# Outer products of one chunk moved behind the first products, two loads swapped, and last groups issued in two rounds

## The chip, the cores and the metric

The kernel runs on one core of a Trainium2 chip. The metric is the device time of one execution in microseconds (us). The engines of the core are TensorE (PE, matrix products and weight loads), VectorE (DVE), ScalarE (ACT), GpSimd (POOL) and SyncE (SP, which here only issues DMA transfers). Each takes its own instructions strictly in the order of the program and waits on semaphores of the others. Products are summed in PSUM, which is divided into eight banks.

## The reference

A linear attention with decay (a retention recurrence), followed by a two-layer network with the Mish function between the layers:

```python
# q, k, v: (4 batches, 8 heads, 768 steps, 64)
for t in range(S):
    state = gamma[None, :, None, None] * state + np.einsum('bhd,bhe->bhde', k[:, :, t], v[:, :, t])
    y[:, :, t] = scale * np.einsum('bhd,bhde->bhe', q[:, :, t], state)
# x: (3072 tokens, 512); w_in: (512, 2048); w_out: (2048, 512)
h = x @ w_in
sp = np.where(h > 20.0, h, np.log1p(np.exp(np.minimum(h, 20.0))))
g = h * np.tanh(sp)
return (g @ w_out).astype(np.float32)
```

Inputs and output are float32; the kernel works on float16 copies and sums in float32.

## The kernel before, in words

**Chunks and blocks.** The recurrence is computed in 24 chunks of 128 steps (six per batch). Within a chunk the scores of k and q are formed, masked on DVE to the causal half and multiplied by v ("present", L303 and L469); what came before enters through a state, the decayed sum of the outer products of k and v, multiplied by q ("past", L314 and L452). The chunks are grouped in blocks: the first block has four chunks (512 tokens), each further one two (256 tokens). A block's attention output is copied by ACT into a tile `xt`, and then goes through both layers: first products with `w_in` into `h_ps`, Mish on ACT, second products with `w_out` into `o_ps`. From the second block on both layers use seven products for eight, with sums formed on DVE (`x_sums`, `sums_a`, `hsum`, `gsum`, `tmat`).

**The first block** (`first_block`) works on pairs of chunks with two interleaved tokens in each partition, so that one chunk's tokens lie in 64 of the 128 partitions: chunk 0 (or 2) in the lower half, chunk 1 (or 3) in the upper. `outer_first(s)` forms the outer products of both chunks of pair s with 16 products of 64 rows, the two chunks by turns (L291), into one PSUM tile `u_ps` for each chunk. `state_first(g)` adds the previous state with a product by the identity (L299) and lets DVE multiply by the decay (L301), which gives the state of chunk g. `first_g1(h_ps, u, s)` computes half (256 tokens) of the first product u, four products of 128x256 each (L810). Products 0 to 3 take the first slice of `w_in` and are done by halves, so that the first halves can start once the first two chunks' `xt` is there; products 4 to 15 are whole (`g1`, L527).

**Weights.** Each of `w_in` and `w_out` comes in four slices of 1 MB in float32 (`load_w`), in staging tiles of which there are few; a staging tile is loaded anew when its casts are done. `cast_win` (L174) and `cast_wout` (L182 on DVE, L184 on ACT) make the float16 copies. The casts of `w_in` slices 1 to 3 stand on DVE behind the state of chunk 3. The last slice of `w_out` comes in two halves (`load_last_wout`, L168), behind the q and v of chunks 4 and 5 in the order in which SP issues. The staging tiles' release makes SP wait: the second slice of `w_out` needs the tile of `w_in` slice 1.

**Order.** The order of each engine's instructions is the order in which the code issues them (a manual schedule). PSUM tiles with the tag "mm" share four banks; a new tile takes a bank that an earlier one has given up, and its first product waits for that tile's last reader. Tiles with the tag "at" share the other two slots of two banks each.

**The end of the first block** (`first_g2`) forms four output groups, one per chunk, in four PSUM tiles (`t0[0]`, `t1[0]`, `t0[1]`, `t1[1]`). `end(p, i, half)` adds to a group the products of half of the last slice of `w_out` (L1009, two products of 128x512), and `ended(p, i)` adds on DVE (L1015, L1017) and copies on ACT (L1018) what goes to the output. `y_two(1, False)` forms the attention output of the second block, whose `xt` ACT copies at L512, and `outer_two(1)` the outer products that the next blocks need. What follows is the first layer of the second block (`g1_seven`, L642 and L666), for which four sums `x_sums` (L615 to L618) are made on DVE.

Of the kernel before, what the change touches and what calls it, by code (L numbers as in the profile page):

```python
# [10 lines left out]
FP32 = mybir.dt.float32  # L11
# [5 lines left out]
def kernel(  # L17
# [9 lines left out]
    nc = tc.nc  # L27
    B, H, S, D = q.shape
    d_model, d_ff = moe_w_in.shape
    P = 128  # L30
# [3 lines left out]
    HP = H // 2  # L34
    TB = 512
    CPB = TB // C
# [7 lines left out]
    FPS = NFB // NSL  # L44
# [24 lines left out]
    mmps = ctx.enter_context(  # L69
        tc.tile_pool(name="rn_mmps", bufs=4, space=bass.MemoryType.PSUM))  # L70
# [46 lines left out]
    raw, k16s, v16s, t16s, kts, amf = {}, {}, {}, {}, {}, {}  # L117
# [18 lines left out]
    def load_one(g, n, queue):  # L136
        b, c = divmod(g, NCH)
        queue.dma_start(
            loaded[g][n], (q, k, v)[n][b, :, c * C:(c + 1) * C].rearrange("h p d -> p h d"))
# [26 lines left out]
    def load_last_wout(half):  # L166
        f = slice(half * (FPS // 2), (half + 1) * (FPS // 2))
        nc.sync.dma_start(  # L168
            wtmps["out", NSL - 1][:, f], wout_ap[:, NFB - FPS + f.start:NFB - FPS + f.stop])
# [91 lines left out]
    def toks(c):  # L261
        return slice(c * HB, (c + 1) * HB)
# [19 lines left out]
            tri_first.rearrange("p r t -> p (r t)").unsqueeze(1).broadcast_to(  # L282
                (P, HP, R * C)), op=ALU.mult)

    def outer_first(s):
        us[s] = [mmps.tile([P, HP, P], FP32, name="u_ps", tag="mm") for _ in range(2)]
        for i in range(HP):
            half, j = divmod(i, HP // 2)
            for r in range(R):
                for c in range(2):  # L290
                    nc.tensor.matmul(  # L291
                        us[s][c][:, i], k16s[s][toks(c), half, r, 2 * j:2 * j + 2],
                        v16s[s, half][toks(c), r, 2 * j:2 * j + 2],
                        start=i == 0 and r == 0, stop=r == R - 1, skip_group_check=True)

    def state_first(g):
        u = us[g // 2][g % 2]
        if g > 0:
            nc.tensor.matmul(u, ident, states[g - 1], start=False, stop=True, skip_group_check=True)  # L299
        states[g] = stp.tile([P, HP, P], FP16, name="st")  # L300
        nc.vector.tensor_tensor(states[g], u, gcm, op=ALU.mult)  # L301
# [192 lines left out]
    def outer_two(blk):  # L494
        gs = handed_on(blk)
        if gs:
            u_ps = u_tile()
        for j, g in enumerate(gs):
            outer(g, u_ps[:, j, :, :D])
# [35 lines left out]
    def mish(blk, u, h_ps):  # L535
        nt = BLOCKS[blk] * C
        per = TB // nt
        room = NFB * TB // (2 * nt)
        at0, lies = divmod(u * per, room)
        if lies == 0:  # L540
            gtiles[blk, at0] = gp.tile([P, room, nt], FP16, name="g", tag="g0" if blk == 0 else "g")
        gt = gtiles[blk, at0][:, lies:lies + per]
        nc.scalar.activation(gt, h_ps, AF.Mish, scale=inv_boost3)
        for j in range(per):
            gts[blk, u * per + j] = gt[:, j]
# [244 lines left out]
    def load_weights():  # L790
        for s in range(NSL):
            load_w("in", s)
        for s in range(NSL):
            load_w("out", s)
        room(CPB)
        room(CPB + 1)
        for g in (CPB, CPB + 1):
            load_one(g, 0, nc.sync)
            load_one(g, 2, nc.sync)

    def load_more():
        load_last_wout(0)
        load_last_wout(1)
        nload[0] += 2
        load_to(CPB + 4)

    def first_g1(h_ps, u, s):
        t = slice(s * TB // 2, (s + 1) * TB // 2)
        for bp in range(NBP):
            nc.tensor.matmul(  # L810
                h_ps[:, 0, t], win(0, u, bp), xts[0][:, 2 * s:2 * s + 2, bp],
                start=bp == 0, stop=bp == NBP - 1, skip_group_check=True)

    def first_block():
        qf = load_first_q()
        for s in range(2):
            for nm in "kv":
                for half in range(2):
                    load_two(nm, s, half)
        nload[0] = CPB  # L820
        load_weights()
        xts[0] = xtp.tile([P, CPB, HP, C], FP16, name="xt")

        at = at_tile()
        spin_wide(at, HP)
        spin_wide(at, HP)
        spin(at, 8)
        tq = turn_first_q(qf, 0)
        spin_wide(at, 3)
        first_q_out(0, tq, nc.scalar)  # L830
        tq = [tq, turn_first_q(qf, 1)]
        cast_two("k", 0, 0)
        turn_two(0, 0)
        first_q_out(1, tq[1], nc.vector)
        turned_two(0, 0)
        cast_two("k", 0, 1)
        spin_wide(at, 3)
        scores_half(0, 0, at)
        mask_half(0, 0, at)
        turn_two(0, 1)  # L840
        turned_two(0, 1)
        for half in range(2):
            cast_two("v", 0, half)
        at = at_tile()
        spin_wide(at, 3)
        scores_half(0, 1, at)
        mask_half(0, 1, at)
        cast_two("k", 1, 0)
        turn_two(1, 0)
        turned_two(1, 0)  # L850
        cast_two("k", 1, 1)
        outer_first(0)
        state_first(0)
        at = at_tile()
        scores_half(1, 0, at)
        mask_half(1, 0, at)
        y = atps.tile([P, 2, HP, C], FP32, name="y_ps", tag="at")
        present_first(0, y, range(HP))
        turn_two(1, 1)
        turned_two(1, 1)  # L860
        state_first(1)
        past_first(1, y)
        xt_out(0, y)
        for half in range(2):
            cast_two("v", 1, half)
        cast_win(0, 0, nc.gpsimd)
        at = at_tile()
        scores_half(1, 1, at)
        mask_half(1, 1, at)
        y = atps.tile([P, 2, HP, C], FP32, name="y_ps", tag="at")  # L870
        outer_first(1)
        state_first(2)
        h_ps = [mmps.tile([P, 1, TB], FP32, name="h_ps", tag="mm") for _ in range(2)]
        present_first(1, y, range(HP))
        first_g1(h_ps[0], 0, 0)
        past_first(2, y)
        past_first(3, y)
        xt_out(2, y)
        first_g1(h_ps[1], 1, 0)
        cast_win(0, 1, nc.vector)  # L880
        state_first(3)
        for u in range(2, FPS):
            h_ps.append(mmps.tile([P, 1, TB], FP32, name="h_ps", tag="mm"))
            first_g1(h_ps[u], u, 0)
        for u in range(FPS):
            first_g1(h_ps[u], u, 1)
            mish(0, u, h_ps[u])
        for s in range(1, NSL):
            for half in range(2):
                cast_win(s, half, nc.vector)  # L890
            if s == 2:
                late.extend(win_sums())
            if s >= 2:
                some_late(4)
        room_for_sums()
        late.extend(weight_sums(0) + weight_sums(1))
        plan = {9: [(cast_wout, 0), (room_for_more,), (bring_first,)],
                10: [(some_late, 1)],
                12: [(g_sum, 1), (g_sum, 2), (cast_wout, 1), (room_for_more,), (g_sum, 3)],
                16: [(load_more,)]}  # L900
        for u in range(FPS, NFB):
            g1(0, u)
            for fn, *args in plan.get(u + 1, ()):
                fn(*args)
        first_g2()
        hsnaps.append(gp.tile([P, 4, TB], FP32, name="hsnap", tag="g0"))

# [20 lines left out]
    def first_g2():  # L928
        hf = d_model // 2
        pairs = range(CPB // 2)  # L930
# [76 lines left out]
        def end(p, i, half):  # L1007
            for f in range(2 * half, 2 * half + 2):
                nc.tensor.matmul(  # L1009
                    (t0, t1)[i][p], a(p, i, 3)(f), wouts[3][:, f], start=False,  # L1010
                    stop=f == FPS - 1, skip_group_check=True)

        def ended(p, i):
            if i == 0:
                nc.vector.tensor_tensor(osb[p][0], t0[p], osb[p][0], op=ALU.add)  # L1015
            else:
                nc.vector.tensor_tensor(osb[p][1][:, 1], pz[p], osb[p][1][:, 1], op=ALU.add)  # L1017
                nc.scalar.copy(osb[p][1][:, 0], px[p])  # L1018
            row0 = (2 * p + i) * P
            stores.append((1, out[row0:row0 + P], osb[p][i].rearrange("p j c -> p (j c)")))  # L1020

        end(0, 0, 0)
        end(0, 1, 0)
        end(0, 0, 1)
        ended(0, 0)
        end(0, 1, 1)
        ended(0, 1)
        y_two(1, False)
        for half in range(2):
            end(1, 0, half)  # L1030
        ended(1, 0)
        outer_two(1)
        for half in range(2):
            end(1, 1, half)
        ended(1, 1)

    def turn_and_load(g):
        if g < NCK:
# [95 lines left out]
```

## Time and profile before

| | |
|---|---|
| median of 3 runs | 200.24 us (200.23 to 200.88) |
| the profiled execution's own time | 199.78 us |
| its span, first to last instruction | 197.8 us |
| granted TensorE clock | 1.00 |
| PE busy | 189.3 us (96%) |
| DVE / ACT / POOL busy | 143.2 / 105.5 / 91.7 us |
| mean DMA rate | 182 GB/s; about 385 GB/s from 18 to 30 us |

All times in the text are counted from the first instruction of the span. The last chain of work, followed back from the end, lies on PE for 86% of the span. A product's row in the timeline has a modelled end, so the spacing of products is read from their starts. The issue of a DMA and its landing are two things: a landing is the last update of the transfer's semaphore.

### The profile page before, as it was taken

Reading aid. Unit: us, or ns where it says so; the run is one execution under the profiler, and the core shown is the slowest. Engines: PE = TensorE matmul, PEld = TensorE weight load, DVE = VectorE, ACT = ScalarE, POOL = GpSimd, SP = SyncE. Lnnn points to the kernel's source line nnn. Section 1 sums busy time; section 2 is a strip of 40 time slices with the busy share of each in tenths; the row PEclk is TensorE's granted clock in tenths of the full one; section 3 lists DMA queues with packets and bytes.
Section 4 is the critical chain, followed back from the end, with each engine's and each line's share of the span. In section 5 each row is a group of like instructions: output and inputs, shape, how many; then the busy total and the mean of one; then the engine's idle time right before and its main releaser. Section 6 shows DMA issues by size and latency. Waiting matters only on the chain.

```text
span 197.8 us, 5839 instructions
## 1 busy us (share of the span) xinstructions
PE 189.3 (96%) x2431; PEld 157.2 (79%) x2431; DVE 143.2 (72%) x293; ACT 105.5 (53%) x191; POOL 91.7 (46%) x125
## 2 busy tenths in 40 slices
PE   6797999999999999999999999999999999999992
PEld 2355645885988988988988988988988988988982
DVE  3786699778897697597498597597498596596362
ACT  3464577444663663663663753753753753753840
POOL 4072006597663929719707809808716814110000
PEclk9999999999999999999999999999999999999999
DMA  5999999999999999999999995996997974101102
GB/s 170 303 311 376 383 388 302 191 300 165 157 195 204 260 220 210 156 153 214 195 174 111 200 174 128 167 174 149 182 182 123 166 125 97 68 2 56 53 30 80
DMA packets 95658, 36.06 MB, mean 182 GB/s; under 512 B 82576, under 2 KB 89232, under 8 KB 95632
## 3 DMA queue, kind: packets, MB, share of 16 engines
q1 hardware_dynamic: 74400, 33.04, 74.8%
q0 software_dynamic: 21088, 2.62, 21.6%
q8 instruction: 19, 0.31, 0.6%
q14 instruction: 7, 0.06, 0.1%
q10 hardware_dynamic: 144, 0.03, 0.1%
HBM read 27.30 MB, written 6.29 MB: 170 GB/s over the span
## 4 chain that ended last, share of the span: by engine, by line
PE 86%; DVE 6%; DMA 2%; ACT 2%; issue 2%; DVEq 0%
PE o_ps L739 29%; PE h_ps L666 17%; PE h_ps L642 15%; PE h_ps L527 5%; PE o_ps L953 5%; PE y_ps L474 3%; PE at L404 3%; DMA qfirst<-in_q_dram 2%; PE o_ps L1009 2%; PE h_ps L810 2%; PE y_ps L465 1%; DVE st L301 1%; PE u_ps L419 1%; DVE am L279 1%; DVE gsum L585 1%
## 5 line engine op out<-in xcount | busy, mean ns | idle before, releaser
L666 PE MATMUL h_ps<-xt,win 128*128 128x256 f16 x320 | 41.6, 273 | 0.0
L659 DVE TENSOR_TENSOR hsum<-h_ps,hsnap 128x512 f32<-128x512 f32 x30 | 19.8, 688 | 20.8 <-PE h_ps L642 16.9
L739 PEld LDWEIGHTS <-gsum 128*128 128x128 f16 x320 | 30.5, 98 | 4.5
L666 PEld LDWEIGHTS <-win 128*128 128x128 f16 x320 | 29.3, 98 | 3.6
L349 POOL DMA_DIRECT2D qk<-in_k_dram x36 | 27.9, 778 | 0.0
L739 PE MATMUL o_ps<-tmat,gsum 128*128 128x256 f16 x240 | 27.9, 273 | 0.0
L739 PEld LDWEIGHTS <-g 128*128 128x128 f16 x240 | 23.4, 98 | 2.8
L653 ACT ACTIVATE g<-hsum 128x512 f16<-128x512 f32 x30 | 18.6, 630 | 11.4 <-DVE hsum L659 11.2
L410 DVE TENSOR_TENSOR am<-at,tri 128x1024 f16<-128x1024 f32 x20 | 24.3, 1216 | 0.0
L673 ACT ACTIVATE g<-h_ps 128x512 f16<-128x512 f32 x40 | 22.8, 599 | 2.4 <-PE h_ps L666 2.4
L354 POOL TENSOR_TENSOR v<-vf,qvs 128x512 f16<-128x512 f32 x20 | 23.5, 1176 | 1.1 <-DMA vf<-in_v_dram 0.7
L745 ACT COPY snap<-o_ps 128x256 f32<-128x256 f32 x30 | 11.2, 373 | 21.7 <-PE o_ps L739 21.6
L649 ACT COPY hsnap<-h_ps 128x512 f32<-128x512 f32 x30 | 16.4, 582 | 11.5 <-PE h_ps L642 11.5
L362 POOL COPY gate<-gsum 128x1 f16<-128x1 f16 x9 | 1.7, 188 | 44.3 <-DVE gsum L713 40.1
L337 POOL TENSOR_TENSOR qk<-qf,qvs 128x512 f16<-128x512 f32 x20 | 21.2, 1062 | 0.7 <-DMA qf<-in_q_dram 0.6
L753 DVE TENSOR_TENSOR osb<-o_ps,snap 128x256 f32<-128x256 f32 x30 | 12.6, 419 | 12.2 <-PE o_ps L739 10.8
L642 PEld LDWEIGHTS <-wsum 128*128 128x128 f16 x320 | 19.5, 98 | 0.5
L739 PE MATMUL o_ps<-wout,g 128*128 128x256 f16 x160 | 19.3, 273 | 0.0
L512 ACT CAST xt<-y_ps 128x1024 f16<-128x1024 f32 x10 | 10.1, 1013 | 14.6 <-PE y_ps L465 14.6
L642 PE MATMUL h_ps<-xsum,wsum 128*128 128x128 f16 x240 | 16.7, 219 | 0.0
L642 PEld LDWEIGHTS <-win 128*128 128x128 f16 x240 | 15.1, 98 | 0.7
L585 DVE TENSOR_TENSOR gsum<-g 128x256 f16<-128x256 f16 (+1 forms) x30 | 10.7, 358 | 3.8 <-ACT g L653 3.6
(120 smaller groups left out, 294.6 us busy)
## 6 DMA issues: line engine op xcount, KB each, us to landing
vf<-in_v_dram SPq DMA_DIRECT2D x24, 256.0 KB, 6.0
out_dram<-osb SPq DMA_DIRECT2D x22, 256.0 KB, 4.6
qf<-in_q_dram SPq DMA_DIRECT2D x20, 256.0 KB, 5.5
wi<-in_moe_w_in_dram SPq DMA_DIRECT2D x3, 1024.0 KB, 11.3
wt<-in_moe_w_out_dram SPq DMA_DIRECT2D x3, 1024.0 KB, 10.9
qk<-in_k_dram POOLq DMA_DIRECT2D x36, 64.0 KB, 4.9
qfirst<-in_q_dram SPq DMA_DIRECT2D x2, 512.0 KB, 5.0
kf<-in_k_dram SPq DMA_DIRECT2D x4, 256.0 KB, 5.8
```

What stands on the lines that cost most here:

```text
L337: nc.gpsimd.tensor_tensor(by_head(g, room16(g)[0]), by_head(0, loaded[g][0]), f.broadcast_to((P, 2, HP, D)), op=ALU.mult)
L349: nc.gpsimd.dma_start(room16(g)[1][:, x::2], src[:, HP * x:HP * x + HP])
L354: nc.gpsimd.tensor_tensor(room16(g)[2], loaded[g][2], vs.unsqueeze(2).broadcast_to((P, H, D)), op=ALU.mult)
L410: nc.vector.tensor_tensor(am, ats.pop(g), tri.unsqueeze(1).unsqueeze(1).broadcast_to((P, 2, HP, C)), op=ALU.mult)
L585: nc.vector.tensor_tensor(s1, a21, a22, op=ALU.add)
L642: nc.tensor.matmul(h_ps[:, f], w(f, d), x(d), start=first and f == 0 and d == 0, stop=d == n - 1, skip_group_check=True)
L649: nc.scalar.copy(x, h_ps)
L653: nc.scalar.activation(gt[:, 2 * i * FPS:(2 * i + 1) * FPS, j * P:(j + 1) * P], h, AF.Mish, scale=inv_boost3)
L659: nc.vector.tensor_tensor(h, h_ps, x, op=ALU.add)
L666: nc.tensor.matmul(h_ps[:, j], win(s, 2 * half + j, bp), xt(blk, bp), start=bp == 0, stop=bp == NBP - 1)
L673: nc.scalar.activation(gt[:, fb:fb + 2], h_ps, AF.Mish, scale=inv_boost3)
L739: nc.tensor.matmul(o_ps, x(f), w(f), start=first and f == 0, stop=f == n - 1, skip_group_check=True)
```

## The change

`outer_first` takes a list of chunks and can form one chunk's outer products alone. For the second pair of the first block, chunk 2's eight products and its state stay where they were; chunk 3's products and state move behind all halves of the first products 0 to 3. Between them the order becomes: present, past of chunks 2 and 3, the copy of `xt`, first halves of products 0 to 3, second halves with their Mish, chunk 3's outer products, its state, and then the casts of the `w_in` slices 1 to 3 as before. Before, the first half of product 0 stood ahead of the past, that of product 1 behind it, then the state of chunk 3, then the halves of products 2 and 3.

Among the loads the first half of the last `w_out` slice changes places with v of chunk 5. At the end of the first block all four groups take the first half of the last slice, then comes `y_two(1, False)`, then all four take the second half and are ended, with `outer_two(1)` between the second and the third.

```diff
-    def outer_first(s):
-        us[s] = [mmps.tile([P, HP, P], FP32, name="u_ps", tag="mm") for _ in range(2)]
+    def outer_first(s, chunks=(0, 1)):
+        u_ps = {c: mmps.tile([P, HP, P], FP32, name="u_ps", tag="mm") for c in chunks}
         for i in range(HP):
             half, j = divmod(i, HP // 2)
             for r in range(R):
-                for c in range(2):
+                for c in chunks:
                     nc.tensor.matmul(
-                        us[s][c][:, i], k16s[s][toks(c), half, r, 2 * j:2 * j + 2],
+                        u_ps[c][:, i], k16s[s][toks(c), half, r, 2 * j:2 * j + 2],
                         v16s[s, half][toks(c), r, 2 * j:2 * j + 2],
                         start=i == 0 and r == 0, stop=r == R - 1, skip_group_check=True)
+        for c in chunks:
+            us[2 * s + c] = u_ps[c]
...
-        for g in (CPB, CPB + 1):
-            load_one(g, 0, nc.sync)
-            load_one(g, 2, nc.sync)
+        load_one(CPB, 0, nc.sync)
+        load_one(CPB, 2, nc.sync)
+        load_one(CPB + 1, 0, nc.sync)
 
     def load_more():
         load_last_wout(0)
+        load_one(CPB + 1, 2, nc.sync)
         load_last_wout(1)
...
-        outer_first(1)
+        outer_first(1, [0])
         state_first(2)
         h_ps = [mmps.tile([P, 1, TB], FP32, name="h_ps", tag="mm") for _ in range(2)]
         present_first(1, y, range(HP))
-        first_g1(h_ps[0], 0, 0)
         past_first(2, y)
         past_first(3, y)
         xt_out(2, y)
-        first_g1(h_ps[1], 1, 0)
         cast_win(0, 1, nc.vector)
-        state_first(3)
-        for u in range(2, FPS):
-            h_ps.append(mmps.tile([P, 1, TB], FP32, name="h_ps", tag="mm"))
+        for u in range(FPS):
+            if u >= 2:
+                h_ps.append(mmps.tile([P, 1, TB], FP32, name="h_ps", tag="mm"))
             first_g1(h_ps[u], u, 0)
         for u in range(FPS):
             first_g1(h_ps[u], u, 1)
             mish(0, u, h_ps[u])
+        outer_first(1, [1])
+        state_first(3)
         for s in range(1, NSL):
             for half in range(2):
                 cast_win(s, half, nc.vector)
...
-        end(0, 0, 0)
-        end(0, 1, 0)
-        end(0, 0, 1)
-        ended(0, 0)
-        end(0, 1, 1)
-        ended(0, 1)
+        ends = [(p, i) for p in pairs for i in range(2)]
+        for p, i in ends:
+            end(p, i, 0)
         y_two(1, False)
-        for half in range(2):
-            end(1, 0, half)
-        ended(1, 0)
-        outer_two(1)
-        for half in range(2):
-            end(1, 1, half)
-        ended(1, 1)
+        for p, i in ends:
+            if (p, i) == (1, 0):
+                outer_two(1)
+            end(p, i, 1)
+            ended(p, i)
```

## The prediction

> **What bounds the kernel now.** I read the page first: the span, the busy shares and the chain that ended last.
>
> ```profile
> span 197.8 us, 5839 instructions
> PE 189.3 (96%) x2431; PEld 157.2 (79%) x2431; DVE 143.2 (72%) x293; ACT 105.5 (53%) x191; POOL 91.7 (46%) x125
> q8 instruction: 19, 0.31, 0.6%
> PE 86%; DVE 6%; DMA 2%; ACT 2%; issue 2%; DVEq 0%
> ```
>
> TensorE (PE) is the bound: whatever makes it wait is paid in full, whatever lies on another engine is paid only if PE waits for it. So I went to the timeline of all engines where the change falls (columns: start, duration, what; in brackets the idle time before it and what ended it).
>
> ```profile
> 15.33 0.62 PE L291 MATMUL u_ps<-v,qk 64*128 64x128 f16 x16
> 16.59 0.68 DVE L301 TENSOR_TENSOR st<-u_ps,gcm 128x512 f16<-128x512 f32 x1
> 17.07 0.61 PE L810 MATMUL h_ps<-xt,win 128*128 128x256 f16 x4
> 17.19 0.68 DVE L174 CAST win<-wi 128x1024 f16<-128x1024 f32 x1
> 17.97 0.27 PE L810 MATMUL h_ps<-xt,win 128*128 128x256 f16 x1
> 19.05 0.49 PE L810 MATMUL h_ps<-xt,win 128*128 128x256 f16 x3 [0.81 <-issue]
> 19.38 0.38 PE L299 MATMUL u_ps<-st,ident 128*128 128x512 f16 x1
> 19.79 0.69 DVE L301 TENSOR_TENSOR st<-u_ps,gcm 128x512 f16<-128x512 f32 x1 [1.92 <-PE u_ps L299]
> 20.54 2.34 PE L810 MATMUL h_ps<-xt,win 128*128 128x256 f16 x20 [0.34 <-DVE st L301]
> 20.74 1.29 DVE L174 CAST win<-wi 128x1024 f16<-128x1024 f32 x2 [0.25 <-DMA wi<-in_moe_w_in_dram]
> 22.72 0.59 PE L527 MATMUL h_ps<-xt,win 128*128 128x512 f16 x2
> ```
>
> Two PE stalls stand here: a start-to-start gap of 1.08 us (17.97 to 19.05, "issue": no semaphore), and one before 20.54, where the fourth product needs the PSUM bank that the state of chunk 3 has just been read from. See also the order on VectorE (DVE): state, then the two casts of weight slice 1, done at 22.03, 0.7 us before L527 needs them at 22.72. From there to 58 us PE has no stall over 0.2 us. Next SyncE's issues, and the stretch at the end of the first block:
>
> ```profile
> 17.95 5.03 SPq L163 DMA_DIRECT2D wt<-in_moe_w_out_dram  x3
> 34.15 0.96 SPq L138 DMA_DIRECT2D vf<-in_v_dram  x1
> 35.16 2.09 SPq L168 DMA_DIRECT2D wt<-in_moe_w_out_dram  x2
> 44.60 1.05 ACT L184 CAST wout<-wt 128x1024 f16<-128x1024 f32 x1 [0.42 <-DMA wt<-in_moe_w_out_dram]
> 44.72 2.00 PE L1009 MATMUL o_ps<-wout,g 128*128 128x512 f16 x8
> ```
>
> The eight products start 0.216 us apart but for the fifth, the first that needs the second half of the last output slice: that half is cast only at 45.65, and the product starts at 45.70 instead of 45.59. This 0.1 us is all that the loading order costs PE.
>
> **What the issue gap is.** PE has 4871 records and queue q8 moved 19 packets, 0.31 MB: 16 KB, so 256 instructions of 64 bytes, each. In the trace the first q8 packet moves at 16.49 to 17.58, when DMA is full (385 GB/s), and the later ones begin where PE's records number about 950, 1250, 1544, 1767: one block of 256 each. The gap falls behind record 448. I read it as a block of instructions landing late, usable at 19.05 whatever is in it. The Trainium skill, "Runtime: NRT & Kernel Launch", Instruction fetch mechanics, says that an engine fetches blocks of 256 instructions by itself and that crossing a block is mostly hidden; the size agrees with the trace, the hiding does not at this place, if my reading holds. By that rule the gap would be something else; that is the first rival.
>
> **The change, part by part.** All from the profiled execution (199.78 us, span 197.8 and 1.98 around it); its time lies 0.46 below the median of 200.24.
>
> *Outer products split.* The 16 products of half rows (64x128) alternate between the two chunks, and start every 28 ns. The eight of chunk 2 alone stay where they were. The trace shows no run of one half alone: low bound 28 ns (0.22 us), high bound 98 ns (a weight load each, 0.78). I take 56 ns, the row of full-height products of the same width (L642, 16 in 0.89): 0.45. For chunk 2 this costs nothing: outer and state product end by 16.1, and present waits for the mask until 16.73 either way. The Trainium skill, "TensorEngine Tiling (Array Packing)", Key Properties, says that different tiles compute in parallel and that each is tied to its partitions; by it one half alone loses the overlap, 0.45 as taken here and not 0.22, and it speaks against this split.
>
> *The new order on PE.* Present ends, next kind starts at 17.07 as before. The past products come at once (8, 0.45: 17.52); xt's second half is copied from about 17.7 to 18.7, before it is needed. Products 0, 1, 2 of first halves: 12 by 0.109, to 18.83. There record 448 is reached again (8 pairs fewer from the outer products, 8 more first halves), and PE waits to 19.05: 0.2 us where 1.08 stood. Product 3 and the second halves: 20 by 0.109, to 21.23. The bank wait of 0.34 is gone. Chunk 3's outer products: a switch of kind (148 ns against 56, so 0.09), 0.45, another 0.09: the state product starts at 21.86. Their bank was one of the four products': product 0's activation ends by 20.8, no wait; if it is product 3's, some 0.6 more (its activation ends at about 22.0). I take the first, free soonest.
>
> *What is late next.* DVE runs in order, and the state of chunk 3 now waits for a product 2.5 us later than before (19.38 to 21.86), with the casts of slice 1 queued behind it. State product to DVE 0.41 (19.38 to 19.79): 22.27. Next DVE instruction 0.60 later (16.59 to 17.19), cast 0.68: 23.55, release 0.05 (20.48 to 20.54): L527 starts at 23.60 instead of 22.72, **+0.88**. With the bounds of the outer products, +0.65 to +1.21.
>
> *Behind the casts.* The casts of slice 2 start 0.6 later; their users on PE come 3.5 us after L527, so hidden; DVE catches up at 34.38 and 36.37, where it idled 0.39 (a DMA) and 1.08 (ScalarE, ACT). SyncE (SP) issues the second output slice only when both casts of slice 1 are done: 22.06 becomes about 24.2. Ahead of it in the queue lie the last input slice (landed 26.1) and the first output slice (28.8), so its landing at 31.55 holds; were that cover gone it would land up to 2.1 later and be cast by 34.9, still ahead of PE's first use of it at 35.7. The q and v loads behind it were held back by a full queue to 34.1 and catch up.
>
> *Loads swapped.* The first half of the last output slice lands about 1.2 us earlier (43.1 to 41.9: v of chunk 5 took 39.34 to 40.50), v of chunk 5 some 2.6 later (40.5 to 43.1). GpSimd (POOL) takes v of chunk 5 at 43.14, now 44.0: hidden by 0.9. The second half lands as before, 44.6.
>
> *Two rounds.* The same products and switches; the second round starts after y_two, 2.9 us later, so the 0.1 wait goes: **-0.10**. The copy of xt leaves from behind the last groups and comes sooner, with nothing waiting for it. On DVE the four sums now follow y_two closely: counted from its end, the fourth starts 2.43 us later instead of 2.27, and xsum 0.16 later. DVE idles 0.24 before 54.01, which hides that. Chunk 3's state is ready 20 us ahead of its next reader (L446, 44.5).
>
> Sum: +0.88 - 0.10 = **+0.78**; nothing behind it gives any back, since PE and the DVE chain of 54 to 62 us both shift. 199.78 becomes 200.56; on the median, 201.0.
>
> **Rivals.**
> 1. *The pause goes with the instructions, not with the clock* (or the block is asked for later): PE stops 1.08 at record 448, so 19.80 instead of 19.05, +0.75 more: 201.8, slower by over 0.5%. Decides once PE resumes after about 19.3. For it: "issue" names no cause. Against: the q8 packets.
> 2. *The casts hold nothing up*: PE goes from the state product (21.86 and 0.22) straight to L527: 22.08, -0.64, with -0.10 and so 199.5, faster. It decides if the casts of slice 1 end before 22.03. For it: the weights landed by 20.7, DVE is idle from 17.9. Against: DVE's rows stand in the order of the code, and there the state stays ahead of the casts.
> 3. *DVE becomes the bound in block 1*: if the third sum waits for ACT's copy (one such wait of 0.5 is listed), xsum is 0.48 late, 0.24 over its cover, and PE, which already waits 0.2 for the mask at 61.95, pays it: 201.3.
>
> **How the numbers follow.** Forecast 0.60, rival 1 0.15, rival 2 0.13, rival 3 0.12. About 0.5% (1.0 us) is what a measurement can tell from no change. The forecast's own range is +0.55 to +1.11: 200.8 to 201.35. The range goes down to 200.1 for the 0.65 by which the three runs differ, and up to 201.9 to take in rivals 1 and 3; it leaves out rival 2 and some ends. Slower by over 0.5% (from 201.24): rival 1, half of rival 3, and 0.10 of the forecast's upper end, 0.31. Faster by over 0.5% (199.24): the lower part of rival 2, 0.05. Within: 0.64.
>
> **What would show it.** L527's first product at 23.6 behind a DVE cast, DVE idle from 17.9 to 22.3, the "issue" gap near 0.2 and ending at 19.05, the bank wait gone; SP's second output slice at 24.2 with its landing unmoved; no gap in L1009; PE's wait at 62 as before. The prediction is wrong if the issue gap is long at another place, if the casts come ahead of the state, or if a wait appears behind 45 us.

## The result and the profile after

The changed kernel takes 201.14 us (median), the kernel before 200.19 us beside it: a ratio of 1.0053 with an interval of [1.0034, 1.0073]. It is slower, by 0.95 us between the medians; 201.0 was predicted. The ratio is of means, without two slow executions of the changed kernel (203.62 and 204.61). The profiled execution of the changed kernel took 200.51 us (span 198.6), the least of its 22; that of the kernel before took 199.78 (span 197.8). That is 0.73 more, where the sum of the prediction was 0.78.

In the new code the lines have moved by two or three: L299 is now L301 (state product), L301 L303 (state on DVE), L527 L529 (whole first products), L642 L644, L666 L668, L739 L741, L810 L813, L1009 L1012, L1017 L1020, L1018 L1021.

The page's first line, and its chain that ended last by engine: the instructions are as many as before, and PE's share of the chain went from 86% to 90%, while "issue" went from 2% to 1%.

```profile
span 198.6 us, 5839 instructions
PE 90%; DVE 3%; DMA 2%; ACT 1%; issue 1%; DVEq 0%
```

The timeline after, PE and DVE, where chunk 3's outer products now stand (start, duration, what, and in brackets the idle time before it and its releaser):

```profile
17.52 3.76 PE L813 MATMUL h_ps<-xt,win 128*128 128x256 f16 x32
21.77 0.39 PE L301 MATMUL u_ps<-st,ident 128*128 128x512 f16 x1
22.19 0.69 DVE L303 TENSOR_TENSOR st<-u_ps,gcm 128x512 f16<-128x512 f32 x1 [4.36 <-PE u_ps L301]
22.80 2.49 DVE L174 CAST win<-wi 128x1024 f16<-128x1024 f32 x4
23.54 0.82 PE L529 MATMUL h_ps<-xt,win 128*128 128x512 f16 x3 [1.39 <-DVE win L174]
```

The 32 half products run as one group from 17.52; the two stalls of before (1.08 at the block of instructions, 0.34 at the bank) have left one start-to-start gap, 18.84 to 19.05, inside that group. But DVE then stands idle for 4.36 us, because the state of chunk 3 is next in its order, and the casts behind it end so late that PE waits 1.39 us in front of L529. PE's two small stalls were traded for one large one.

At the end of the first block the eight products of the first half (L1012) now run from 45.55 without a gap. What follows in the timeline of after (PE, DVE, ACT):

```profile
50.52 1.06 PE L644 MATMUL h_ps<-xt,win 128*128 128x128 f16 x16
50.97 0.41 DVE L1020 TENSOR_TENSOR osb<-o_ps,osb 128x256 f32<-128x256 f32 x1
51.41 0.37 ACT L1021 COPY osb<-o_ps 128x256 f32<-128x256 f32 x1 [0.84 <-DVE osb L1020]
51.68 0.59 ACT L651 COPY hsnap<-h_ps 128x512 f32<-128x512 f32 x1
52.31 0.69 DVE L661 TENSOR_TENSOR hsum<-h_ps,hsnap 128x512 f32<-128x512 f32 x1
57.37 1.04 PE L741 MATMUL o_ps<-wout,g 128*128 128x256 f16 x8
```

The same stretch in the timeline of before, for comparison:

```profile
49.76 1.06 PE L642 MATMUL h_ps<-xt,win 128*128 128x128 f16 x16
49.95 0.42 DVE L1017 TENSOR_TENSOR osb<-o_ps,osb 128x256 f32<-128x256 f32 x1 [0.45 <-PE o_ps L1009]
50.41 0.37 ACT L1018 COPY osb<-o_ps 128x256 f32<-128x256 f32 x1 [0.79 <-DVE osb L1017]
51.31 0.69 DVE L659 TENSOR_TENSOR hsum<-h_ps,hsnap 128x512 f32<-128x512 f32 x1
```

Between the first product of this layer and the first of the next lie 6.62 us before (49.76 to 56.38) and 6.85 after (50.52 to 57.37). Four small gaps make the difference, each before a product whose semaphores wait for DVE or ACT: 0.04 at 52.33, 0.10 at 54.19, 0.04 at 54.68 and 0.055 at 55.17 (of the two groups of eight there, the starts are 0.49 apart where 0.44 stood). `hsum`, the first sum over a finished `h_ps`, starts 1.79 us behind the first L644; before it was 1.55. Both numbers are the start of the last group's sum (0.45 behind the first L644, 0.20 behind the first L642 before) and 1.34 or 1.35 us more. The last sum is late because it follows the third group's sum on DVE without a pause (its row has no idle time), where DVE had idled 0.45 before.

Two ways lead from the last sum to `hsum`, and they are nearly equally long. ACT's copy and then `hsnap` end at 52.28, and `hsum` follows at 52.31. On DVE itself the four x sums stand between; they are spaced about 0.20 us (the last two start at 51.83 and 52.03), so by an estimate DVE alone would have begun `hsum` at 52.23, still 0.16 later against PE than before.

The balance at a product that both share, the fourth group of L741 (62.82 before, 63.69 after): 0.82 at L529, less 0.10 at L1012, plus 0.24 in these gaps, less 0.11 because the wait for the mask at 62 fell from 0.23 to 0.12. That is 0.85 of the 0.87, and the span is 0.8 longer. The next run shows which edit each of these belongs to.

### The profile page after: what moved, and what is told of

Its sections match the earlier page's. It is cut to its first block, busy times and chain, and to the rows that moved or that the text cites. A ratio compares the mean times of both kernels' runs of the same rounds, so it can differ in the third digit from the quotient of the medians.

```text
span 198.6 us, 5839 instructions
## 1 busy us (share of the span) xinstructions
PE 190.6 (96%) x2431; PEld 157.8 (79%) x2431; DVE 143.0 (72%) x293; ACT 105.5 (53%) x191; POOL 91.7 (46%) x125
## 4 chain that ended last, share of the span: by engine, by line
PE 90%; DVE 3%; DMA 2%; ACT 1%; issue 1%; DVEq 0%
PE o_ps L741 31%; PE h_ps L668 18%; PE h_ps L644 16%; PE h_ps L529 5%; PE o_ps L956 5%; PE y_ps L476 3%; PE at L406 3%; DMA qfirst<-in_q_dram 2%; PE o_ps L1012 2%; PE h_ps L813 2%; PE y_ps L467 1%; DVE st L303 1%; PE u_ps L421 1%; DVE am L279 1%; DVE qfirst L209 1%
## 5 line engine op out<-in xcount | busy, mean ns | idle before, releaser
L668 PE MATMUL h_ps<-xt,win 128*128 128x256 f16 x320 | 41.6, 273 | 0.0
L741 PEld LDWEIGHTS <-gsum 128*128 128x128 f16 x320 | 30.6, 98 | 4.4
L668 PEld LDWEIGHTS <-win 128*128 128x128 f16 x320 | 29.3, 98 | 3.6
L741 PE MATMUL o_ps<-tmat,gsum 128*128 128x256 f16 x240 | 27.9, 273 | 0.0
L741 PEld LDWEIGHTS <-g 128*128 128x128 f16 x240 | 23.4, 98 | 2.8
L675 ACT ACTIVATE g<-h_ps 128x512 f16<-128x512 f32 x40 | 22.8, 600 | 2.4 <-PE h_ps L668 2.4
L356 POOL TENSOR_TENSOR v<-vf,qvs 128x512 f16<-128x512 f32 x20 | 24.0, 1199 | 0.0
L339 POOL TENSOR_TENSOR qk<-qf,qvs 128x512 f16<-128x512 f32 x20 | 21.3, 1064 | 0.0
L644 PEld LDWEIGHTS <-wsum 128*128 128x128 f16 x320 | 19.6, 98 | 0.6
L741 PE MATMUL o_ps<-wout,g 128*128 128x256 f16 x160 | 19.3, 273 | 0.0
L644 PE MATMUL h_ps<-xsum,wsum 128*128 128x128 f16 x240 | 16.7, 219 | 0.0
L644 PEld LDWEIGHTS <-win 128*128 128x128 f16 x240 | 15.1, 98 | 0.7
L545 ACT ACTIVATE g<-h_ps 128x512 f16<-128x512 f32 x16 | 9.2, 598 | 6.7 <-PE h_ps L529 5.5
```

The lines of the kernel that those rows point to most:

```text
L339: nc.gpsimd.tensor_tensor(by_head(g, room16(g)[0]), by_head(0, loaded[g][0]), f.broadcast_to((P, 2, HP, D)), op=ALU.mult)
L356: nc.gpsimd.tensor_tensor(room16(g)[2], loaded[g][2], vs.unsqueeze(2).broadcast_to((P, H, D)), op=ALU.mult)
L644: nc.tensor.matmul(h_ps[:, f], w(f, d), x(d), start=first and f == 0 and d == 0, stop=d == n - 1, skip_group_check=True)
L668: nc.tensor.matmul(h_ps[:, j], win(s, 2 * half + j, bp), xt(blk, bp), start=bp == 0, stop=bp == NBP - 1)
L675: nc.scalar.activation(gt[:, fb:fb + 2], h_ps, AF.Mish, scale=inv_boost3)
L741: nc.tensor.matmul(o_ps, x(f), w(f), start=first and f == 0, stop=f == n - 1, skip_group_check=True)
```

## The experiments

Executions of one kernel differ here by one to three us, so beside each ratio the profiled execution's marks are given; they can be compared from mark to mark. Where not said otherwise the kernel is the changed one with one more edit.

**Outer products alone.** The loads and the end of the block as before, only `outer_first`, `state_first(3)` and the order of the halves as in the change.

```diff
...
-        ends = [(p, i) for p in pairs for i in range(2)]
-        for p, i in ends:
-            end(p, i, 0)
...
+        end(0, 0, 0)
+        end(0, 1, 0)
+        end(0, 0, 1)
+        ended(0, 0)
...
+        ended(1, 1)
```

> Only the outer products of chunk 3 are moved; the loads and the last groups are as before. Theory (the state of chunk 3 holds the casts of weight slice 1 back on DVE): the first whole product (L527 of before) starts 0.85 us later than in the kernel before (about 23.55 against 22.72), the pause without a cause is 0.1 long and ends at 19.05, and the time is 0.8 to 0.9 us longer than before, 0.1 longer than that of the whole change. Rival (the loss lies in the loads or in the two rounds): this kernel is as fast as before.

Measured: ratio 1.0067 [1.0034, 1.0099] (201.59 against 200.08; profiled execution 200.35, span 198.4). In its timeline DVE stands idle for 4.31 ahead of the state, as after, and then PE:

```profile
23.54 1.68 PE L529 MATMUL h_ps<-xt,win 128*128 128x512 f16 x7 [1.38 <-DVE win L174]
```

The whole loss at L529 is there, and the gaps behind 50 us are not: 6.62 (50.56 to 57.18) from the first L644 to the first L741, as before. So the loss at L529 belongs to the moved outer products and the gaps to the two rounds. The two small gains are not the two rounds' either: here too the eight products at the end of the first block run without a gap from 45.55, and the wait for the mask at 62 is 0.10. PE comes 0.83 us later to the last output slice, so its second half is ready in time. The fourth group of L741 starts at 63.48, which is 0.66 later than before and 0.21 earlier than in the changed kernel: at this mark the two rounds only cost. The ratios of the two kernels are too close to tell them apart.

**All but the outer products.** The reverse: the swapped loads and the two rounds, with the first block as before.

```diff
-        outer_first(1, [0])
+        outer_first(1)
         state_first(2)
...
+        first_g1(h_ps[0], 0, 0)
...
+        first_g1(h_ps[1], 1, 0)
...
-        outer_first(1, [1])
-        state_first(3)
```

> Only the load swap and the two rounds; the first block's order is as before. Theory: PE's timeline up to 44.7 us is that of the kernel before, the gap of 0.1 us at the fifth product of the last groups is gone, and the time is 0.1 us shorter (199.7 where before takes 199.8 in its profile). Rival (the two rounds or the later v cost something behind 45 us): 0.3 us longer or more, with a wait on PE behind y_two.

Measured: ratio 1.0005 [0.9971, 1.0040] (199.83 against 200.08), no difference; neither the 0.1 gained nor the 0.24 lost in the two rounds could show in an interval this wide. Its profiled execution (201.74) was one of the long ones: all of its start is later by 0.8. The order of the marks holds: no gap in L1012, the same four gaps (53.26, 55.12, 55.61, 56.10), and 7.08 us from the first L644 to the first L741, of which 0.235 is a wait of its own at 57.21. The rest is 6.85, as after. Two readings come from its timeline (the product ahead of the gap started at 18.77):

```profile
19.82 0.49 PE L813 MATMUL h_ps<-xt,win 128*128 128x256 f16 x3 [0.78 <-issue]
46.46 1.06 POOL L339 TENSOR_TENSOR qk<-qf,qvs 128x512 f16<-128x512 f32 x1
46.99 2.09 DVE L452 TENSOR_TENSOR st<-su,gcm 128x512 f16<-128x512 f32 x1
47.47 1.05 POOL L356 TENSOR_TENSOR v<-vf,qvs 128x512 f16<-128x512 f32 x1
49.14 0.40 PE L458 MATMUL y_ps<-qkt,st 128*128 128x128 f16 x4 [0.85 <-DVE st L452]
```

The issue gap ends at 19.82 instead of 19.05, later by as much as the rest of the start: it is not tied to a fixed time, as the prediction had it, but moves with the start of the execution. The four other lines are taken up at the end.

**Casts ahead of the state.** The changed kernel with the two casts of weight slice 1 ahead of chunk 3's outer products, so that DVE does not wait for the state first.

```diff
+        for half in range(2):
+            cast_win(1, half, nc.vector)
         outer_first(1, [1])
         state_first(3)
         for s in range(1, NSL):
             for half in range(2):
-                cast_win(s, half, nc.vector)
+                if s > 1:
+                    cast_win(s, half, nc.vector)
```

> The whole change, but on DVE the two casts of weight slice 1 stand ahead of the state of chunk 3. Theory: PE goes from chunk 3's state product straight to the first whole product, at 22.0 to 22.1 us in place of 23.54; SP issues the second output slice at 22.3 again; the time is 0.7 us shorter than before (0.64 there and 0.10 at the last groups) and 1.5 us shorter than with the change. Rival (PE is held by something else there, a block of instructions or the PSUM bank): the first whole product stays near 23.5.

Measured: ratio 0.9995 [0.9964, 1.0026] (200.05 against 200.08; profiled execution 199.44, span 197.6). Its timeline, DVE, PE and POOL:

```profile
20.55 1.30 DVE L174 CAST win<-wi 128x1024 f16<-128x1024 f32 x2 [2.79 <-DMA wi<-in_moe_w_in_dram]
21.82 1.46 PE L529 MATMUL h_ps<-xt,win 128*128 128x512 f16 x6
47.25 1.04 POOL L356 TENSOR_TENSOR v<-vf,qvs 128x512 f16<-128x512 f32 x1 [0.34 <-DMA vf<-in_v_dram]
48.34 0.32 PE L421 MATMUL u_ps<-v,qk 128*64 128x64 f16 x8 [0.63 <-POOL v L356]
```

With the casts ahead, DVE waits for the weights (20.55) and not for the state, L529 follows the state product (21.59) with no wait, and it starts 1.72 us earlier than in the changed kernel, 0.90 earlier than before. So it is the order on DVE that holds PE up. But the 0.90 did not reach the end: `outer_two` (L421) needs v of chunk 6, whose load landed at 47.11 (47.08 before), and PE, now ahead of the loads, waited 0.63 for it; then came the gaps of the two rounds (0.24).

**More records ahead.** The kernel before, with 16 small products of no meaning behind its warm-up products, 32 records on PE (each product has a weight load). If the gap stands at a fixed record, it moves onto an instruction 16 products earlier; if it hangs on the instruction, it stays with it.

```diff
+        for _ in range(16):
+            spin(at, 1)
```

> The kernel before with 16 more small products in the warm-up at 5 us, where PE waits for q anyway: 32 more PE records ahead of everything. If the pause of 1.08 us is a block of 256 instructions that lands by the clock, it falls 32 records earlier in the program, in the middle of the second present (about 16.9 us), still ends at about 19.05, and what PE did from 16.9 to 17.97 comes behind it: the first whole product starts about 1.0 us later (23.7) and the time is 1.0 us longer than before. If the pause belongs to the product of L810, it stays there, with 1.08 us, and the time is that of before.

Measured: ratio 1.0074 [1.0040, 1.0108] (201.89 against 200.08; profiled execution 201.35). Its timeline of PE around the gap:

```profile
17.04 0.90 PE L309 MATMUL y_ps<-am,v 64*64 64x128 f16 x29
19.27 0.25 PE L309 MATMUL y_ps<-am,v 64*64 64x128 f16 x3 [1.33 <-issue]
```

The gap has moved into L309, and the half products at L810 run through; the first L527 came at 24.12. Counted in records it is where it was: in this kernel, the one before, the changed one and the one without the move, PE stops ahead of the 449th record or so, with 223 products begun in each. A gap of instruction supply explains that, a property of the product at L810 does not. Its time is no price of 32 records: the granted clock was full only from 6.82 us (4.79 before), the first of the added products started 107 ns apart until then and the rest 56, and they pushed the whole start back by 0.8 us; and PE, which reaches the 449th record 0.24 earlier than before (17.73 for 17.97), stops for 1.54 from start to start.

In the four traces, PE executes its 193rd record or so at 13.19, 13.15, 13.98 and 13.37 us, and the gap ends at 19.05, 19.05, 19.82 and 19.27: 5.86, 5.90, 5.84 and 5.90 later. 449 less 193 is 256, one block of 16 KB. I read it so: a block is asked for when the block two before it has been used up, and with DMA at 385 GB/s it takes 5.9 us to be usable. Three more of the traces here stop at that record, if only for 0.03 to 0.18 us, and in all seven the interval is 5.83 to 5.98; in the other four PE comes there 5.79 to 5.80 us after the 193rd record and does not stop. So the interval is nearly constant, but not to 0.1 us. That the 193rd record is what sends the request is argued from the count, and the later packets of q8 bear it out: in the profile before, from the second on, each begins within 71 records of 193 plus a multiple of 256 (507 for 449, 741 for 705, 950 for 961, and so on to 4798 for 4801).

**The x sums first.** The gaps of the two rounds, by the prediction's step, could come from `x_sums` on DVE, which stand behind the four groups' sums. Here they stand ahead of the last group's sum.

```diff
         for p, i in ends:
             if (p, i) == (1, 0):
                 outer_two(1)
             end(p, i, 1)
+            if (p, i) == (1, 1):
+                x_sums(FIRST)
             ended(p, i)
...
-    x_sums(FIRST)
```

> The whole change, with the four xsum instructions on DVE ahead of the end of the fourth group in place of behind it. Theory (the two rounds delay xsum by 0.2, and with it the Mish and the copy on ACT that product groups of block 1 wait for): the four extra waits of PE between 52 and 55.5 us (0.24 in all) go, from the first L644 product to the first L741 product it takes 6.6 us as in the kernel before, not 6.85, and the time is 0.1 to 0.2 us below that of the change. Rival (these waits come from elsewhere): 6.85 stays.

Measured: ratio 1.0094 [1.0062, 1.0125] (202.15 against 200.29; profiled execution 201.58). Its timeline behind the groups:

```profile
51.90 0.42 DVE L1020 TENSOR_TENSOR osb<-o_ps,osb 128x256 f32<-128x256 f32 x1
52.35 0.37 ACT L1021 COPY osb<-o_ps 128x256 f32<-128x256 f32 x1 [1.77 <-DVE osb L1020]
52.62 0.59 ACT L651 COPY hsnap<-h_ps 128x512 f32<-128x512 f32 x1
53.26 1.05 PE L644 MATMUL h_ps<-xsum,wsum 128*128 128x128 f16 x16 [0.81 <-ACT hsnap L651]
```

The theory fell. The x sums came 0.33 earlier and nothing was gained; the last group's sum, which slid from 50.97 to 51.90, took ACT's copy with it, that copy took `hsnap` with it, which stands behind it on ACT; DVE's `hsum` (53.24) waited 0.93 for it and PE 0.81. Here the chain that matters is: last sum on DVE, its copy on ACT, `hsnap` on ACT, `hsum` on DVE. In the changed kernel this chain and the x sums on DVE end within 0.08 us of each other, as worked out above, so taking the x sums out of the way could gain next to nothing there.

**Outer products of the second block last.** From the order with the casts ahead: `outer_two(1)` behind all four groups, four products of 0.216 us later in PE's order, so that v of chunk 6 has time to land.

```diff
         for p, i in ends:
-            if (p, i) == (1, 0):
-                outer_two(1)
             end(p, i, 1)
             ended(p, i)
+        outer_two(1)
```

> The whole change with the casts of slice 1 first, and the outer products of chunks 4 and 5 for the next blocks behind all four groups, not between the second and the third. Theory (the gain of casts_first was given back at these products, which waited 0.7 us for v of chunk 6, landed at 47.1 us whatever PE does): the wait goes, the first L644 product starts at about 48.9 (49.46 in casts_first, 49.81 before), and the time is 0.8 to 0.9 us below that of before. Rival (something else waits for the same transfers): the wait appears again at the next reader, and the time stays within 0.3 us of before.

Measured: ratio 0.9975 [0.9948, 1.0001] (199.52 against 200.29; profiled execution 200.22, in which the start was 0.25 later than with the casts ahead alone). From its timeline, PE, POOL and DVE:

```profile
48.95 1.04 POOL L339 TENSOR_TENSOR qk<-qf,qvs 128x512 f16<-128x512 f32 x1 [0.79 <-DMA qf<-in_q_dram]
49.51 0.64 DVE L617 TENSOR_TENSOR xsum<-xt 128x256 f16<-128x256 f16 x1
57.75 0.40 PE L406 MATMUL at<-qkt 64*128 64x128 f16 x8 [0.54 <-DMA qkt<-qk]
```

The wait for v of chunk 6 is gone (L421 at 48.75, right behind the groups), PE reaches the first L741 at 55.84 instead of 56.38, and there the next load is late: the transposed q and k of chunk 7 (`qkt`) landed at 57.70, where they had landed at 57.2 before (7.1 us after the issue instead of 6.4), and PE waited 0.54. The gaps of 0.22 before L741 are still there, but from another cause: the last group's sum now starts 0.17 behind the first L644, earlier than in the kernel before, and `hsnap` ends at 50.48. It is the first x sum that is late. It takes 0.64 instead of 0.28, while POOL's L339 runs until 49.99; `hsum` follows the x sums at 50.79. At 62.73 little is left of the lead (62.82 before). Putting the x sums early in this order as well gave the harm of the run above again:

```diff
             end(p, i, 1)
+            if (p, i) == (1, 1):
+                x_sums(FIRST)
             ended(p, i)
...
-    x_sums(FIRST)
```

> Both of the two edits on top of the casts first. Theory: the gains add, 1.0 to 1.1 us below before. Rival (the chain on DVE from 54 to 62 us sets the end): no more than outer_last alone.

Measured: ratio 0.9996 [0.9973, 1.0018] (200.17 against 200.29); 7.83 us from the first L644 to the first L741, with PE waiting 0.85 for `hsnap`.

**Ends turned.** If the chain through ACT's copy is what makes the gaps, it is enough to end the group without a copy last: in each pair, the group i = 1 (a sum and a copy) ahead of i = 0 (a sum alone). The order above ran again beside it.

```diff
-        ends = [(p, i) for p in pairs for i in range(2)]
+        ends = [(p, i) for p in pairs for i in (1, 0)]
```

> The order with the casts of slice 1 ahead of chunk 3's outer products and outer_two behind the groups, and in each pair of groups the one with the ACT copy ended first, so that DVE's last sum has no ACT copy behind it. Theory (what follows the last copy on ACT is late): ACT's last copy comes some 0.9 us earlier, counted from the last group, and the three waits of PE that stood at 52.66, 53.15 and 53.65 in the order before it (0.115, 0.044 and 0.056) go: 0.2 us less, about 199.3, ratio 0.996 to 0.998. Rival 1: by then ACT's snapshot already followed PE and not the copy (49.89 against a copy that ended at 49.99), so the waits stay as they are and the time is that of outer_last. Rival 2: the last group's DVE sum is now the long one (0.68 for 0.41), so the four x sums come 0.27 later and the waits grow by up to 0.27.

> The same kernel as outer_last, beside ends_turned on one chip. If its gain over the kernel before is real, the ratio lies again between 0.995 and 1.000 and its profile has L644 near 49.0 and L741 near 55.8 (both shifted by where the clock is released). If it was chance, the ratio is 1.000 to 1.003.

Measured: turned 0.9997 [0.9977, 1.0017] (200.31), unturned 0.9995 [0.9976, 1.0013] (199.79), both against 200.22. The turned order's timeline:

```profile
49.26 0.37 ACT L1024 COPY osb<-o_ps 128x256 f32<-128x256 f32 x1 [0.70 <-DVE osb L1023]
49.74 0.28 DVE L617 TENSOR_TENSOR xsum<-xt 128x256 f16<-128x256 f16 x1
49.85 0.59 ACT L651 COPY hsnap<-h_ps 128x512 f32<-128x512 f32 x1 [0.22 <-PE h_ps L644]
50.67 0.68 DVE L661 TENSOR_TENSOR hsum<-h_ps,hsnap 128x512 f32<-128x512 f32 x1
```

The first L644 starts at 49.14; the copy follows 0.12 later (0.89 after), `hsnap` waits for PE alone, the gaps are gone: 6.63 us to the first L741. The foretold waits went, but this does not show that the copy made them. In the unturned order `hsnap` was not late either, as the first rival said: it started 0.89 behind the first L644, 0.93 in the kernel before. What differs is the first x sum: here it starts at 49.74, when POOL's L339 has ended (49.72), and takes 0.28; in the unturned order it began beside that operation and took 0.64, and 0.58 in the execution that ran again. So the run shows once more that PE pays for a late `hsum`, and that DVE's own x sums can be what makes it late; the ACT copy is shown to do so in the run with the x sums first. A run of the changed kernel with only that copy moved was not made. The gain does not reach the total: PE waits 0.37 for `qkt` (57.50) again, and at the fourth group of L741 the turned order is 0.26 ahead (62.48 against 62.74), which a measurement does not tell from nothing. Nor does the gain of the unturned order against the kernel before repeat: 0.9975 once, 0.9995 the second time. None of these versions is shown to beat the kernel before; against the changed kernel (1.0034 at the lowest) all orders with the casts ahead are faster (1.0026 at the highest).

The marks side by side (us, profiled executions):

| | first L527/L529 | first L642/L644 | first L739/L741 | between these two | first `hsum` behind the first L642/L644 |
|---|---|---|---|---|---|
| before | 22.72 | 49.76 | 56.38 | 6.62 | 1.55 |
| after | 23.54 | 50.52 | 57.37 | 6.85 | 1.79 |
| outer products alone | 23.54 | 50.56 | 57.18 | 6.62 | 1.55 |
| all but them | 23.49 | 51.45 | 58.53 | 7.08 | 1.79 |
| casts ahead | 21.82 | 49.46 | 56.31 | 6.85 | 1.79 |
| more records | 24.12 | 51.09 | 57.94 | 6.85 | 1.56 |
| x sums first | 23.54 | 50.52 | 58.43 | 7.91 | 2.72 |
| `outer_two` last | 22.07 | 49.00 | 55.84 | 6.84 | 1.79 |
| the same again | 22.04 | 48.97 | 55.75 | 6.78 | 1.73 |
| the same, x sums first | 21.48 | 49.17 | 57.00 | 7.83 | 2.77 |
| the same, ends turned | 22.06 | 49.14 | 55.77 | 6.63 | 1.53 |

The last two columns go together: up to about 1.55 the lateness of `hsum` costs nothing, and beyond it PE pays about as much as `hsum` is late. Three rows hold another wait that this does not cover, 0.23 us twice (all but them, more records) and 0.13 once (x sums first): at a later product of the layer (57.21, 56.62 and 57.11), in executions in which a sum for `tmat` on DVE took 1.53 or 1.54 instead of 0.68.

## Why the prediction was right

The time (201.0 against 201.14), the direction and the main mechanism came out. The gain of 0.10 came from another cause than the one named, and two small terms were missed, a loss and a gain; that these nearly cancel with the error of the first term is luck.

- *Casts of slice 1 held up behind the state* (+0.88): +0.82 at L529, and the run with the casts ahead took it away. The steps before it: state product at 21.86 foretold, 21.77 found; DVE's state 22.27, 22.19; the release by the first of the two casts 23.60, 23.54. Rival 2 is out.
- *Outer products of one half at 56 ns each*: the starts of the eight were 56 ns apart, 28 was the paired figure. The half price would have put L529 at 23.3. The Trainium skill, "TensorEngine Tiling (Array Packing)", Key Properties, was given in the prediction for the lost overlap; the trace agrees.
- *The issue gap shrinks and ends at 19.05*: it did, at record 449. The reason given, a block landing by the clock whatever PE does, was wrong: without the move it ended at 19.82. It ends about 5.9 us behind PE's use of an earlier record, and the early part of the kernel was not changed. Rival 1 had the place (a count of records) but not the length: PE reaches record 449 at 18.84 instead of 17.97 and so waits 0.1 where it had waited 1.0.
- *Bank wait gone, chunk 3's bank free*: no wait before 21.21.
- *SP's second output slice 2.1 later, its landing held*: issued at 24.11 (24.2 foretold), landed 31.79 against 31.55. The queue held it back, 0.24 short of exactly.
- *Loads swapped, hidden*: first half landed 41.31 (43.11 before; 41.9 foretold), v of chunk 5 at 42.30 (43.1 foretold), POOL's cast of it at 43.98 (44.0 foretold). PE waits for neither.
- *Two rounds −0.10*: L1012 without a gap, as foretold, but not for the reason given. With the outer products alone, without the two rounds, the gap was not there either. The second half landed at 43.90 there; but even the landing of before, cast at 45.65, would have done, because the fifth product starts only at 46.43 when PE is 0.83 late. The prediction added the two terms as if each stood alone, but a kernel that comes 0.8 late does not meet that wait. The size was right by luck.
- *xsum 0.16 later, hidden by DVE's idle 0.24 before 54.01*: this step failed. The fourth sum came 0.25 later against PE (0.20 behind the first L642 before, 0.45 after), and the cover that was named lies in front of the second `hsum`. The first one had no cover. It was late by both ways, the x sums on DVE and ACT's copy with `hsnap`, and ACT's was the later by an estimated 0.08; the prediction had ACT only as a wait of DVE. It cost 0.24. Rival 3 had the size (0.24) and another cause.
- *PE's wait for the mask at 62 as before*: it fell by 0.11, and by 0.13 with the outer products alone, so this gain belongs to them and not to the two rounds.
- *Nothing behind gives any back*: not quite true for the loss, of which the 0.10 at the last slice and the 0.11 at the mask came back. For the gains of the experiments it is false: they came to lie ahead of the loads.

So +0.82 − 0.10 + 0.24 − 0.11 stands where +0.88 − 0.10 was forecast: the missed terms add 0.13, of which the first term, 0.06 too large, hides half.

## What to carry to other kernels

When a product is moved later on PE, look at what stands behind its consumer on the next engine: here the state of one chunk, needed 20 us later, held two casts that PE needed at once, and moving it behind them took the whole loss away. When a sequence is regrouped, measure the lateness of each side engine's step against the first product that follows, and look for the first buffer release that this delays, not for idle time somewhere further on. When two gains or losses lie on the same engine, ask whether the first leaves the second in place: a wait for a load of 0.1 is gone by itself once everything ahead of it is 0.8 late. A lead on PE is worth only as much as the loads allow: 0.9 us won at 22 us was stopped by one load at 48 and by another at 57.

## What the runs showed of the hardware

**Instructions come late when DMA is full.** From start to start PE stood 1.08 us (before) to 1.54 (with more records) at record 449, and in seven traces the gap ended 5.83 to 5.98 us after record 193. In these seven the first packet of q8 begins 3.2 to 3.5 us after that record and moves for about 1.1 us, and PE goes on 1.3 to 1.5 us after its end. The Trainium skill, "Runtime: NRT & Kernel Launch", Instruction fetch mechanics, calls the crossing of a block mostly hidden and gives PE a buffer of 2048 instructions; its other sentence, on a store of two blocks, fits these traces better, in which PE runs out 256 records after the first block's end. In the profile before, PE showed no other gap of this kind up to 58 us.

**DVE waits for POOL as a whole.** L452 reads two operands from SBUF and takes 0.68 us by itself. In the trace without the move, quoted there, POOL had begun at 46.46 and followed with a second operation at 47.47: DVE's row begins at 46.99 and lasts 2.09, so its last 0.68 begin at 48.40, about when POOL's second operation ends (48.52 by its row). With one POOL operation in its way it lasted 1.09 (after) to 1.51 (`outer_two` last with the x sums first); when DVE began first (casts ahead, 45.32 against 45.54) it took 0.68 and POOL 1.37 instead of 1.04. The first x sum is a second case: 0.28 alone, 0.58 to 0.64 beside POOL's L339. The Trainium skill, "SBUF — State Buffer", SBUF: two separate sides, has it as a lock that is held for the whole instruction; the rows agree. Who comes next differs between executions: without the move DVE was not served between two POOL operations that follow closely, but after the change and with the outer products alone, where they follow as closely, it was (1.09 and 1.14), and POOL's second operation took 1.51 and 1.56. The long row cost PE 0.85 us in the execution without the move, about as much as the whole change.

**The start differs from execution to execution.** In the eleven traces PE's granted clock became full at 4.75 to 7.99 us, and stayed so for 191.15 or 194.56 us, 56 or 57 times 3.413. The Trainium skill, "TensorE: Matmul & The Clock Gate", What's actually happening, describes a window of 3.413 us that runs freely; the lengths agree. How much of the spread of one to three us among executions this makes, and how much the first loads, stays open.
